# Sorting the first of five transpose tasks of each attention head one slot group later, in a kernel of attention, a routed expert layer and a max of three linear maps

## The chip, the core and the metric

The kernel runs on one core of a Trainium2 chip. The metric is the device time of one execution in microseconds (us). Five engines work side by side, each through its own queue in order: TensorE (PE: matmuls and transposes; its weight loads are listed as PEld), VectorE (DVE), ScalarE (ACT), GpSimd (POOL) and SyncE (SP, which issues DMA transfers). An engine that reaches an instruction whose input is not ready waits there, and all that is queued behind it waits too. Transfers are also issued by GpSimd (the indirect ones, which gather rows by a list of indices).

## The reference

All data is fp32. The sizes are batch 4, 8 heads, 576 positions, head size 64; a token is one position of one batch, 2304 in all, of 512 elements.

```
scores = q k^T / 8 + cum[i] - cum[j]          cum = cumsum(log f), causal
attn   = exp(scores - rowmax) / rowsum        out = attn v
x      = out as 2304 tokens of 512 (8 heads x 64)
e      = argmax over 8 experts of cosine(x, expert_emb) / tau, gate = its softmax weight
x      = gate * (relu(x w1[e]) w2[e])         512 -> 1024 -> 512
h      = max(x m1, x m2, x m3)                512 -> 768
result = h w_out                              768 -> 512
```

## The kernel before

**Heads and row blocks.** The 32 heads (4 batches x 8) are taken two at a time as 16 pairs p; head h is 2p or 2p+1. The 576 rows of a head are cut into row blocks t = 0 to 4. Block 0 holds the last 64 rows left over and is made for both heads of a pair at once; block t = 1 to 4 has 128 rows and, being causal, 128 t + 64 columns: 192, 320, 448 and 576. For each block, TensorE makes the scores (`s_h_t_k`, lines 421 and 426, two passes each; block 4 in two halves of 288 columns), VectorE adds the mask and takes the row extreme (`P_h_t` and `nm`, lines 448 and 454), ScalarE makes the exponential in place with its row sum (line 480), TensorE transposes the block in squares of 128 (`t_h_t<-swap,P_h_t`, line 500), and ScalarE or VectorE evicts the squares to `PT` (`PT<-t`, lines 535 for VectorE and 537 for ScalarE).

**The remainders.** The 64 columns of each block beyond the squares of 128 are transposed apart, all four of a head into one tile of its own, `tl_h` (one buffer). Those of blocks 1 to 3 stand in the same task as that block's squares and ahead of them (line 498, `tl_h<-ident,P_h_t`). The one of block 4 is a task by itself, called t = 0 in the code (line 494, `tl_h<-ident,P_h_4`): it allocates the tile, and the tasks of blocks 1 to 3 name it as something they come after. When all four are in, one eviction copies them to `PT` (`PT<-tl_h`).

**After a pair.** VectorE adds up the row sums (`sum_p`, line 547). GpSimd copies them with the two halves of the partitions exchanged (`rs_p`, lines 552 and 553), and VectorE takes the reciprocal of `rs_p` in place (line 556). TensorE multiplies by V (`po_p_u`, line 570, u = 0 and 1), the result is evicted (`ot_p_u`), transposed back by a matmul (`pb_p_u`, line 590), and VectorE multiplies it by the reciprocal (line 599). SP stores it to `x_dram` (line 610).

**The early expert.** One expert's share of the tokens of the first three batches is worked on before all of attention is done. A small matmul, `p3` (line 886), counts; ten small VectorE instructions on its result (lines 889 to 917) end in a list of indices, `gidxe`; GpSimd gathers the rows (two indirect transfers `V0<-x_dram,gidxe`, line 645), SP loads that expert's weights (`we0`, `we1` and a spare tile, line 682), VectorE and ScalarE split the weights into a rounded part and the rest (into `At1`, `Bt1`, `R11`, `R21`, `At2`, `Bt2`, lines 535, 537 and 690), TensorE transposes the gathered rows (`xe`, line 651, evicted to `xs0` and `xs1`), and `pe0` (line 1239) is the first matmul of the expert stage. Later gathers of the other experts' tokens are called `gat` (line 1405).

**What sets the order.** Nothing of attention is written in the order in which it is issued. Each step is a task with a list of engines that may do it, an estimated cost, a priority, the tasks it comes after and the buffers it needs. A small greedy scheduler in the kernel's own code (class `Sched`) keeps a clock for each engine in its estimates; again and again it takes, of the tasks that are ready, the one that can start first by its clocks, and among those that can start alike the one with the lowest priority. The program is emitted in that order. The buffers that it counts are three for score tiles `s`, two for transposed squares `t`, one for `tl`, two for `po` and `pb` together, eight for `P`. Priorities are slots: `slot[h, t]` is 5 h + i for the i-th of the order 4, 0, 3, 1, 2, scores have `slot - 2`, transposes have `slot + 3` (`LT` is 3), a pair's closing steps have 10 p + 20 and a little more.

Of the kernel before, what the change touches and what calls it, by code (L numbers as in the profile page):

```python
# [266 lines left out]
def attention(tc, g, qT, kT, v, x_dram, es):  # L267
# [79 lines left out]
    sd = Sched({"s": 3, "P": NPB, "t": 2, "tl": 1, "o": 2, "ot": 2}, 9.0)  # L347
# [5 lines left out]
    LEAD, LT, LO = 2, 3, 10  # L353
    order = (4, 0, 3, 1, 2)
    slot = {(h, t): 5 * h + i for h in range(NH) for i, t in enumerate(order)}
    side, ready, fs, fr, fe, ft, fv, ftv, fo, fb, fn_ = {}, {0: []}, {}, {}, {}, {}, {}, {}, {}, {}, {}
# [55 lines left out]
    def s_task(h, t, k, j0, w):  # L412
        p, r = divmod(h, 2)
        i = p % NQ

        def fn(e):
            st = st_[h, t, k] = ps_s.tile([128, 512], F32, tag="s", name=f"s_{h}_{t}_{k}")
            wp = max(w, 192)
            for ps_i, (lt, rt, kk) in enumerate(((At[i], R1[i], 128), (Bt[i] if p else At[i], R2[i], 66 if p else 128))):
                if t == 0:  # L420
                    nc.tensor.matmul(st[:, 0:192].rearrange("p (r j) -> p r j", r=2), lt[0:kk].rearrange("p r q -> p (r q)")[:, S - 64:S + 64],
                                     rt[0:kk, :, 0:96],
                                     start=(ps_i == 0), stop=(p > 0 and ps_i == 1))
                    continue
                q0 = ROW0[t] - (0 if r else 64)
                nc.tensor.matmul(st[:, 0:wp], lt[0:kk, r, q0:q0 + 128],  # L426
                                 rt[0:kk, r, j0:j0 + wp], start=(ps_i == 0), stop=(p > 0 and ps_i == 1))
            if p == 0 and t == 0:
                for x in range(2):
                    nc.tensor.matmul(st[:, 96 * x:96 * x + 96], g.pick[:, x], g.cc[:, 0:96], start=False, stop=(x == 1))  # L430
            elif p == 0:
                nc.tensor.matmul(st[:, 0:wp], g.pick[:, r], g.cc[:, j0:j0 + wp], start=False, stop=True)

        fs[h, t, k] = sd.task("PE", pe(2 * max(w, 192)), fn, slot[h, t] - LEAD, side.get(h, []), get=("s", (h, t, k)))

    def r_task(h, t, k, j0, w, n, ext):
        def fn(e):
            if k == 0:
                if t == order[0] and h % H == 0:
                    b = h // H  # L440
                    sums[b] = sm.tile([128, NBLK, H], F32, tag="sums", name=f"sums{b}", bufs=2)
                    nc.vector.memset(sums[b][:, 0, :], 1.0)
                P = pp.tile([128, S], F32, tag="P", name=f"P_{h}_{t}")
                nm = sm.tile([128, 2], F32, tag="nm", name=f"nm_{h}_{t}")
                Pt[h, t] = P, nm
            P, nm = Pt[h, t]
            if t == 0:
                nc.vector.tensor_tensor_reduce(out=P[:, 0:128].rearrange("p (r j) -> p r j", r=2),
                                               in0=st_.pop((h, t, k))[:, 0:192].rearrange("p (r j) -> p r j", r=2)[:, :, 0:64],
                                               in1=g.mask2, scale=-0.125, scalar=3.0e38, op0=ALU.add, op1=ALU.min,  # L450
                                               accum_out=nm[:, 0:1])
                return
            m0 = S - ext + j0
            nc.vector.tensor_tensor_reduce(out=P[0:n, j0:j0 + w], in0=st_.pop((h, t, k))[0:n, 0:w], in1=g.mask[0:n, m0:m0 + w],  # L454
                                           scale=-0.125, scalar=(3.0e38 if k == 0 else nm[0:n, 0:1]),
                                           op0=ALU.add, op1=ALU.min, accum_out=nm[0:n, k:k + 1])

        deps = [fs[h, t, k]] + ([fr[h, t]] if k else [])
        fr[h, t] = sd.task("DVE", dve(w), fn, slot[h, t], deps, get=None if k else ("P", (h, t)), rel=[("s", (h, t, k))])
# [3 lines left out]
    def head(h):  # L463
        p, r = divmod(h, 2)
        b = h // H
        T = PT[h % NPT]
        for t in order:
            n, ext = ROWS[t], EXT[t]
            if t == 0:
                n, ext = 128, 128  # L470
                if r == 0:
                    continue
            parts = ((0, 288), (288, 288)) if t == 4 else ((0, ext),)
            for k, (j0, w) in enumerate(parts):
                s_task(h, t, k, j0, w)
                r_task(h, t, k, j0, w, n, ext)

            def exp(e, t=t, n=n, ext=ext, k=len(parts) - 1, c=h % H):
                P, nm = Pt[h, t]
                nc.scalar.activation(out=P[0:n, 0:ext], in_=P[0:n, 0:ext], func=AF.Exp, bias=nm[0:n, k:k + 1], scale=-1.0,  # L480
                                     accum_out=sums[b][0:n, t, c:c + 1])

            fe[h, t] = sd.task("ACT", 0.28 + ext / 1200, exp, slot[h, t], [fr[h, t]])
            if t == 0:
                fe[h - 1, 0], fs[h - 1, 0, 0] = fe[h, 0], fs[h, 0, 0]
        old = [fo[p - 2]] if p >= 2 else []
        for t in order:
            i0 = ROW0[t]

            def tr(e, t=t, i0=i0):  # L490
                P = Pt.pop((h, t))[0] if t not in (0, 4) else Pt[h, 4][0]
                if t == 0:
                    tl = tl_[h] = ps_t.tile([128, 512], F32, tag="tl", name=f"tl_{h}", bufs=1)
                    nc.tensor.transpose(tl[0:64, 3 * LAP:4 * LAP], Pt.pop((h, 4))[0][0:LAP, 512:576], g.ident[0:LAP, 0:LAP])
                    return
                w = tl_[h, t] = ps_t.tile([128, 512], F32, tag="t", name=f"t_{h}_{t}")
                if t != 4:
                    nc.tensor.transpose(tl_[h][0:64, LAP * t - LAP:LAP * t], P[0:LAP, 128 * t:128 * t + 64], g.ident[0:LAP, 0:LAP])
                for a in range(t):
                    nc.tensor.transpose(w[:, 128 * a:128 * a + 128], P[:, 128 * a:128 * a + 128], g.swap)  # L500
                if t == 1 and r:
                    nc.tensor.transpose(w[:, 128:256], Pt.pop((h, 0))[0][:, 0:128], g.ident)

            nb = {0: 0.6, 1: 1.6 + r, 2: 2.6, 3: 3.6, 4: 4}[t]
            deps = [fe[h, 4]] if t == 0 else [fe[h, t]] + ([ft[h, 0]] if t != 4 else []) + ([fe[h, 0]] if t == 1 and r else [])
            ft[h, t] = sd.task("PE", 0.107 * nb, tr, slot[h, t] + LT, deps, get=("tl", h) if t == 0 else ("t", (h, t)),
                               rel=[("P", (h, x)) for x in {0: (4,), 1: (0, 1) if r else (1,), 4: ()}.get(t, (t,))])
            if t == 0:
                continue

            def ev(e, t=t, i0=i0):
                w = tl_.pop((h, t))
                if t == 1 and r:
                    for x in range(2):
                        evict(e, PT[(h - 1 + x) % NPT][0:64, 0, 0:64], w[low[x], 128 + 64 * x:192 + 64 * x])
                evict(e, T[:, 0:t, i0:i0 + 128], w[:, 0:128 * t].rearrange("p (a i) -> p a i", a=t))

            x = 0.26 if t == 1 and r else 0.0
            fv[h, t] = sd.task(("ACT", "DVE"), (act(128 * t) + x, dve(128 * t) + x), ev, slot[h, t] + LT - 4, [ft[h, t]] + old,
                               rel=[("t", (h, t))])  # L520

        def tail(e):
            d = T[0:64, 1, 128:192]
            dst = bass.AP(tensor=d.tensor, offset=d.offset, ap=[list(d.ap[0]), [S + 128, 4], [1, 64]])
            evict(e, dst, tl_.pop(h)[0:64, 0:4 * LAP].rearrange("p (a i) -> p a i", i=LAP)[:, :, 0:64])

        fv[h, 0] = sd.task(("ACT", "DVE"), (act(256), dve(256)), tail, slot[h, order[-1]] + LT - 4,
                           [ft[h, t] for t in order] + old, rel=[("tl", h)])
# [4 lines left out]
    def evict(e, out, in_):  # L533
        if e == "DVE":
            nc.vector.tensor_copy(out, in_)  # L535
        else:
            nc.scalar.activation(out=out, in_=in_, func=AF.Copy)
# [1336 lines left out]
```

## Time and profile before

| | before |
|---|---|
| median of 3 runs (lowest to highest) | 723.43 us (723.03 to 724.41) |
| the profiled execution, its own time | 724.2 us |
| its span, first to last instruction | 722.5 us |
| TensorE busy | 98% of the span, 4699 instructions |
| VectorE, ScalarE, GpSimd busy | 60%, 52%, 22% |
| mean granted TensorE clock | 0.998 of full speed |

The trace is of one execution. Busy time is the time in which an engine had at least one instruction under way; a row of the timeline gives the start, the duration, the engine, the line, the operation with what it writes and reads (buffer numbers left out, so that `s_31_3` and `s_30_2` are both `s`), the shapes and a count where alike rows follow each other. In brackets behind it stands how long the engine sat idle just before, and what ended that.

### The profile page before, as it was taken

How to read it: one execution, taken by the hardware profiler on the slowest of the kernel's cores; microseconds unless marked ns; L12 is line 12 of the kernel's file. 1: busy time of each engine (PE TensorE's matmuls, PEld its weight loads, DVE VectorE, ACT ScalarE, POOL GpSimd, SP SyncE). 2: the span in 40 equal slices, each digit the busy share in tenths (PEclk: the TensorE clock that was granted, in tenths of full speed). 3: DMA queues.
4: the chain of work that ended last, by engine and by line, in shares of the span. 5: the costliest groups of instructions: out<-in, count | busy, mean ns of one | idle time of the engine just before them, and what ended most of it. 6: DMA issues, size and time to landing. Idle time of an engine off the chain costs nothing. (4 is left out here: it accounts for less than half of the span.)

```text
span 722.5 us, 12938 instructions
## 1 busy us (share of the span) xinstructions
PE 708.6 (98%) x4699; PEld 642.4 (89%) x4699; DVE 436.8 (60%) x1108; ACT 373.2 (52%) x860; POOL 155.5 (22%) x203
## 2 busy tenths in 40 slices
PE   8999999999999999999999999999999999999996
PEld 7788897888999999999999999888888888888994
DVE  7978988888888987778976779412302221221220
ACT  7899989998577555566565544311211121122111
POOL 7895565741020101102100000100020011002001
PEclk9999999999999999999999999999999999999999
DMA  7779586725366665656656423000010000001001
GB/s 241 240 223 273 133 242 188 200 49 165 95 205 212 213 220 185 216 195 230 194 192 222 164 80 116 30 15 0 1 59 0 1 30 29 1 0 46 14 1 46
DMA packets 44764, 89.77 MB, mean 124 GB/s; under 512 B 23320, under 2 KB 23320, under 8 KB 44696
## 3 DMA queue, kind: packets, MB, share of 16 engines
q1 hardware_dynamic: 41144, 79.10, 34.6%
q0 software_dynamic: 3520, 9.78, 3.9%
q8 instruction: 39, 0.64, 0.4%
q14 instruction: 29, 0.24, 0.1%
q10 hardware_dynamic: 32, 0.02, 0.0%
HBM read 74.87 MB, written 9.44 MB: 117 GB/s over the span
## 5 line engine op out<-in xcount | busy, mean ns | idle before, releaser
L1640 DVE TENSOR_TENSOR tm<-pm,tm 128x512 f32<-128x512 f32 (+1 forms) x60 | 38.3, 638 | 177.9 <-PE pm L1241 177.5
L1241 PE MATMUL pm<-y,m 128*128 128x512 f32 (+1 forms) x288 | 108.1, 375 | 0.0
L1239 PE MATMUL pm<-y,m 128*128 128x512 f32 (+1 forms) x288 | 108.1, 375 | 0.0
L1240 PE MATMUL pm<-y,m 128*128 128x512 f32 (+1 forms) x288 | 108.1, 375 | 0.0
L1682 POOL DMA_INDIRECT out_dram<-oo,ctidx x18 | 17.8, 988 | 336.9 <-ACT oo L1679 333.9
L480 ACT ACTIVATE P<-P,nm 128x576 f32<-128x576 f32 (+2 forms) x144 | 84.0, 587 | 2.8 <-DVE nm L454 1.3
L1295 DVE TENSOR_TENSOR w<-stg,w 128x1024 fp32r<-128x1024 f32 x60 | 73.0, 1221 | 20.3 <-ACT w L1278 19.4
L1278 ACT ACTIVATE g<-tm 128x512 fp32r<-128x512 f32 (+1 forms) x30 | 17.7, 590 | 114.6 <-DVE tm L1640 114.6
L1278 ACT ACTIVATE w<-stg 128x1024 fp32r<-128x1024 f32 x56 | 59.0, 1056 | 21.8 <-DMA stg<-in_w_dram 10.9
L1239 PE MATMUL py<-h,w 128*128 128x256 f32 (+6 forms) x224 | 68.7, 307 | 0.0
L1239 PE MATMUL ph<-x,w 128*128 128x256 f32 (+6 forms) x224 | 67.8, 303 | 0.0
L1240 PE MATMUL ph<-x,w 128*128 128x256 f32 (+6 forms) x224 | 67.7, 302 | 0.0
L1241 PE MATMUL py<-h,w 128*128 128x256 f32 (+6 forms) x224 | 67.6, 302 | 0.0
L1241 PE MATMUL ph<-x,w 128*128 128x256 f32 (+6 forms) x224 | 67.6, 302 | 0.0
L1240 PE MATMUL py<-h,w 128*128 128x256 f32 (+6 forms) x224 | 67.5, 301 | 0.0
L426 PE MATMUL s<-R,At 128*128 128x288 f32 (+3 forms) x170 | 60.2, 368 | 2.4 <-DVE nm L454 1.1
L454 DVE CUSTOM_DVE_ANT_0 P<-s,mask 128x288 f32<-128x288 f32 (+3 forms) x128 | 58.6, 475 | 6.0 <-PE s L426 2.2
L1241 PEld LDWEIGHTS pm<-y,m 128*128 128x128 f32 x288 | 54.1, 188 | 8.5
L1240 PEld LDWEIGHTS pm<-y,m 128*128 128x128 f32 x288 | 54.0, 188 | 8.5
L1239 PEld LDWEIGHTS pm<-y,m 128*128 128x128 f32 x288 | 54.1, 188 | 8.4
L1405 POOL DMA_INDIRECT gat<-x_dram,gidx x20 | 23.3, 1166 | 158.1 <-PE xt L1412 133.4
L500 PE MATMUL t<-swap,P 128*128 128x128 f32 x320 | 55.7, 275 | 0.3 <-DVE PT L535 0.2
(385 smaller groups left out, 1748.7 us busy)
## 6 DMA issues: line engine op xcount, KB each, us to landing
stg<-in_w_dram SPq DMA_DIRECT2D x60, 512.0 KB
sd<-in_m_dram SPq DMA_DIRECT2D x18, 512.0 KB
q<-in_q_dram SPq DMA_DIRECT2D x15, 576.0 KB
k<-in_k_dram SPq DMA_DIRECT2D x15, 576.0 KB
Bt<-At SPq DMA_DIRECT2D x15, 288.0 KB
V<-in_v_dram SPq DMA_DIRECT2D x8, 512.0 KB
x_dram<-XL SPq DMA_DIRECT2D x64, 64.0 KB
sd_o<-in_mo_dram SPq DMA_DIRECT2D x6, 512.0 KB
```

The costliest lines, as they stand in the source:

```text
L426: nc.tensor.matmul(st[:, 0:wp], lt[0:kk, r, q0:q0 + 128], rt[0:kk, r, j0:j0 + wp], start=(ps_i == 0), stop=(p > 0 and ps_i == 1))
L454: nc.vector.tensor_tensor_reduce(out=P[0:n, j0:j0 + w], in0=st_.pop((h, t, k))[0:n, 0:w], in1=g.mask[0:n, m0:m0 + w], scale=-0.125, scalar ...
L480: nc.scalar.activation(out=P[0:n, 0:ext], in_=P[0:n, 0:ext], func=AF.Exp, bias=nm[0:n, k:k + 1], scale=-1.0, accum_out=sums[b][0:n, t, c:c ...
L500: nc.tensor.transpose(w[:, 128 * a:128 * a + 128], P[:, 128 * a:128 * a + 128], g.swap)
L1239: nc.tensor.matmul(out, whi, xhi, start=start, stop=False)
L1240: nc.tensor.matmul(out, whi, xlo, start=False, stop=False)
L1241: nc.tensor.matmul(out, wlo, xhi, start=False, stop=stop)
L1278: nc.scalar.activation(out=out, in_=in_, func=AF.Copy)
L1295: ENG[e].tensor_tensor(out=w[:, 1], in0=t, in1=w[:, 0].bitcast(F32), op=ALU.subtract)
L1405: nc.gpsimd.indirect_dma_start(out=t[0:n], out_offset=None, in_=x_dram, in_offset=bass.IndirectOffsetOnAxis(ap=idx, axis=0))
L1640: nc.vector.tensor_tensor(out=mx[0], in0=mx["p", w][:, 0:MC], in1=mx[0], op=ALU.max)
L1682: nc.gpsimd.indirect_dma_start(out=out, out_offset=bass.IndirectOffsetOnAxis(ap=g.sidx[:, col:col + 1], axis=0), in_=o[1], in_offset=None, ...
```

## The change

The task of block 4's remainder had the priority `slot[h, 0] + 3`, the second of its head. It gets that of block 3's transposes, `slot[h, 3] + 3`, plus 0.2. All the rest of the code is as it was.

```
             nb = {0: 0.6, 1: 1.6 + r, 2: 2.6, 3: 3.6, 4: 4}[t]
             deps = [fe[h, 4]] if t == 0 else [fe[h, t]] + ([ft[h, 0]] if t != 4 else []) + ...
-            ft[h, t] = sd.task("PE", 0.107 * nb, tr, slot[h, t] + LT, deps, get=...
+            ft[h, t] = sd.task("PE", 0.107 * nb, tr, slot[h, t or 3] + LT + (0.2 if t == 0 else 0.0), deps, get=...
```

The order on TensorE, between the scores of head 5 and the transposes of head 4. The number at the end of a name counts tiles. Before:

```order
L421 MATMUL s_5_0_0_638<-R12_127,At2_120 128x192
L421 MATMUL s_5_0_0_638<-R22_130,Bt2_123 128x192
L494 MATMUL tl_4_641<-ident_75,P_4_4_540 64x66
L426 MATMUL s_5_3_0_644<-R12_127,At2_120 128x448
L426 MATMUL s_5_3_0_644<-R22_130,Bt2_123 128x448
L498 MATMUL tl_4_641<-ident_75,P_4_3_560 64x66
L500 MATMUL t_4_3_648<-swap_187,P_4_3_560 128x128 x3
```

The same place of the change:

```order
L421 MATMUL s_5_0_0_638<-R12_127,At2_120 128x192
L421 MATMUL s_5_0_0_638<-R22_130,Bt2_123 128x192
L426 MATMUL s_5_3_0_641<-R12_127,At2_120 128x448
L426 MATMUL s_5_3_0_641<-R22_130,Bt2_123 128x448
L494 MATMUL tl_4_646<-ident_75,P_4_4_540 64x66
L498 MATMUL tl_4_646<-ident_75,P_4_3_560 64x66
L500 MATMUL t_4_3_648<-swap_187,P_4_3_560 128x128 x3
```

The remainder of block 4 moved behind the scores of `s_5_3` and now stands directly ahead of block 3's remainder. Up to head 13 nothing else moves on TensorE; from head 14 on the scheduler's clocks differ enough that other tasks change places as well.

Late in attention, on TensorE, around `p3`. Before:

```order
L426 MATMUL s_29_4_1_2997<-R12_127,At2_120 128x288
L426 MATMUL s_29_4_1_2997<-R22_130,Bt2_123 128x288
L500 MATMUL t_28_4_3003<-swap_187,P_28_4_2912 128x128 x4
L886 LDWEIGHTS ones_793
L886 MATMUL p3_3009<-ohs_799,ones_793 128x8
L421 MATMUL s_29_0_0_3011<-R12_127,At2_120 128x192
L421 MATMUL s_29_0_0_3011<-R22_130,Bt2_123 128x192
L494 MATMUL tl_28_3015<-ident_75,P_28_4_2912 64x66
L426 MATMUL s_29_3_0_3019<-R12_127,At2_120 128x448
L426 MATMUL s_29_3_0_3019<-R22_130,Bt2_123 128x448
```

In the change:

```order
L426 MATMUL s_29_2_0_3046<-R12_127,At2_120 128x320
L426 MATMUL s_29_2_0_3046<-R22_130,Bt2_123 128x320
L426 MATMUL s_30_4_0_3053<-R10_125,At0_118 128x288
L426 MATMUL s_30_4_0_3053<-R20_128,Bt0_121 128x288
L426 MATMUL s_30_4_1_3059<-R10_125,At0_118 128x288
L426 MATMUL s_30_4_1_3059<-R20_128,Bt0_121 128x288
L886 LDWEIGHTS ones_793
L886 MATMUL p3_3062<-ohs_799,ones_793 128x8
L500 MATMUL t_29_4_3067<-swap_187,P_29_4_2941 128x128 x4
```

`p3` moved from between heads 28 and 29 to behind the first scores of head 30: more of attention's matmuls stand ahead of it, and fewer behind it.

On VectorE, around the reciprocal of `rs_14` (pair 14 is heads 28 and 29; a `P` of head 31 is that head's mask and row extreme, and `nm` its second output). Before:

```order
L547 TENSOR_SCALAR sum_14_3197<-sums3_2492 128x10
L448 ISA P_31_0_3200,nm_31_0_3201<-s_31_0_0_3191,mask2_179 128x128
L448 ISA nm_31_0_3201 128x1
L535 CAST At1_119<-we0_3081 128x512
L454 ISA P_31_3_3218,nm_31_3_3219<-s_31_3_0_3194,mask_78 128x448
L454 ISA nm_31_3_3219 128x1
L454 ISA P_31_1_3241,nm_31_1_3242<-s_31_1_0_3203,mask_78 128x192
L454 ISA nm_31_1_3242 128x1
L454 ISA P_31_2_3245,nm_31_2_3246<-s_31_2_0_3215,mask_78 128x320
L454 ISA nm_31_2_3246 128x1
L556 RECIPROCAL rs_14_3206<-rs_14_3206 128x10
L535 CAST At1_119<-we0_3081 128x512
```

In the change:

```order
L547 TENSOR_SCALAR sum_14_3178<-sums3_2503 128x10
L556 RECIPROCAL rs_14_3181<-rs_14_3181 128x10
L535 COPY ot_14_1_3194<-po_14_1_3157 128x256
L535 CAST At1_119<-we0_3137 128x512
L454 ISA P_31_4_3211,nm_31_4_3212<-s_31_4_0_3189,mask_78 128x288
L454 ISA nm_31_4_3212 128x1
L454 ISA P_31_4_3211,nm_31_4_3212<-s_31_4_1_3201,mask_78,nm_31_4_3212 128x288
L454 ISA nm_31_4_3212 128x1
L448 ISA P_31_0_3226,nm_31_0_3227<-s_31_0_0_3214,mask2_179 128x128
L448 ISA nm_31_0_3227 128x1
L690 TENSOR_TENSOR Bt1_122<-we0_3137,At1_119 128x512
```

The reciprocal moved from behind all of head 31's row extremes to ahead of them, directly behind the sum.

On GpSimd the order is the same in both. Here is the change's, with what each waits for in brackets (DMASW are the queues of the indirect transfers, DMAHW those of SP's):

```order
L645 DMA V0_135<-x_dram_65,gidxe_3114 128x512 [waits DMAHW5_49,DMAHW4_49,DMAHW6_49,DMAHW1_49,DMAHW7_49,DMAHW0_49,DVE_49]
L645 DMA V0_135<-x_dram_65,gidxe_3114 128x512
L552 COPY rs_14_3181<-sum_14_3178 64x10 [waits DMASW1_49,DMASW0_49,DVE_49]
L552 COPY rs_14_3181<-sum_14_3178 64x10
L553 COPY rs_14_3181<-sum_14_3178 64x1 [waits Pool_49]
```

What moved is not here: the copy that fills `rs_14` stands behind both gathers and waits for their queues and for VectorE's sum, before and after the change alike.

## Rows read from the trace of the kernel before

**Rows 1.** The page, parts 1 and 5: busy time; the row-extreme group.

```profile
PE 708.6 (98%) x4699; PEld 642.4 (89%) x4699; DVE 436.8 (60%) x1108; ACT 373.2 (52%) x860; POOL 155.5 (22%) x203
...
L454 DVE CUSTOM_DVE_ANT_0 P<-s,mask 128x288 f32<-128x288 f32 (+3 forms) x128 | 58.6, 475 | 6.0 <-PE s L426 2.2
```

**Rows 2.** Timeline of PE: `s_31_3`, `po_14` and the first row of `pe0`.

```profile
173.36 0.39 PE L426 MATMUL s<-R,At 128*128 128x448 f32 x1
...
174.82 2.94 PE L570 MATMUL po<-PT,V 128*64 128x320 f32 x32
...
187.21 0.38 PE L1239 MATMUL pe<-xs,At 128*128 128x256 f32 x1
```

**Rows 3.** Windows of PE: stretch, length, busy (instructions), clock, DMA share, GB/s.

```profile
88.00:160.00 72.00, 70.81 (x650) 1.00 0.62 172
173.36:187.21 13.85, 13.39 (x121) 1.00 0.42 133
```

**Rows 4.** Timeline of POOL, 164 to 180 us.

```profile
167.74 1.24 POOL L645 DMA_INDIRECT V<-x_dram,gidxe  x1 [5.31 <-PE t L500]
169.29 0.95 POOL L645 DMA_INDIRECT V<-x_dram,gidxe  x1 [0.31 <-issue]
176.95 0.43 POOL L552 COPY rs<-sum 64x10 f32<-64x10 f32 x2 [6.71 <-DMA V<-x_dram,gidxe]
```

**Rows 5.** Timeline of DVE: the reciprocal of `rs_14`.

```profile
177.66 0.22 DVE L556 RECIPROCAL rs<-rs 128x10 f32<-128x10 f32 x1 [1.91 <-POOL rs L553]
```

**Rows 6.** Timeline of PE: remainder alone (102 us) and with a pair (112 us).

```profile
102.31 0.60 PE L500 MATMUL t<-swap,P 128*128 128x128 f32 x4
102.75 0.22 PE L494 MATMUL tl<-ident,P 66*64 66x66 f32 x1
...
103.33 0.50 PE L500 MATMUL t<-swap,P 128*128 128x128 f32 x3
...
112.65 0.60 PE L500 MATMUL t<-swap,P 128*128 128x128 f32 x4
...
113.50 0.22 PE L494 MATMUL tl<-ident,P 66*64 66x66 f32 x1
...
113.62 0.50 PE L500 MATMUL t<-swap,P 128*128 128x128 f32 x3
```

**Rows 7.** Timeline of PE from `p3` on.

```profile
164.45 0.17 PE L886 MATMUL p<-ohs,ones 128*128 128x8 f16 x1
164.48 0.33 PE L421 MATMUL s<-R,At 128*128 128x192 f32 x1
...
166.05 0.90 PE L590 MATMUL pb<-w,ot 128*128 128x144 f32 x6
166.78 0.22 PE L498 MATMUL tl<-ident,P 66*64 66x66 f32 x1
...
167.50 0.66 PE L590 MATMUL pb<-w,ot 128*128 128x144 f32 x4
167.90 0.40 PE L426 MATMUL s<-R,At 128*128 128x320 f32 x1
...
168.29 0.22 PE L494 MATMUL tl<-ident,P 66*64 66x66 f32 x1
168.66 0.37 PE L426 MATMUL s<-R,At 128*128 128x288 f32 x1 [0.15 <-DVE nm L454]
...
169.37 0.25 PE L498 MATMUL tl<-ident,P 66*64 66x66 f32 x1
```

**Rows 8.** The tile V's gathers: from issue to landing.

```profile
DMA to landing us min/median/max: 7.5/7.6/7.8
```

**Rows 9.** Timeline of ACT: exp of `P_31_4`, and the eviction of `tl_31`.

```profile
174.81 0.77 ACT L480 ACTIVATE P<-P,nm 128x576 f32<-128x576 f32 x1
...
182.95 0.37 ACT L537 ACTIVATE PT<-tl 64x256 f32<-64x256 f32 x1
```

**Rows 10.** The tile gat, the later gathers: from issue to landing.

```profile
DMA to landing us min/median/max: 3.0/4.5/8.8
```

More of the change, by code (lines that the diff above doesn't have):

```diff
@@ L505, in head @@
             deps = [fe[h, 4]] if t == 0 else [fe[h, t]] + ([ft[h, 0]] if t != 4 else []) + ([fe[h, 0]] if t == 1 and r else [])
-            ft[h, t] = sd.task("PE", 0.107 * nb, tr, slot[h, t] + LT, deps, get=("tl", h) if t == 0 else ("t", (h, t)),
+            ft[h, t] = sd.task("PE", 0.107 * nb, tr, slot[h, t or 3] + LT + (0.2 if t == 0 else 0.0), deps, get=("tl", h) if t == 0 else ("t", (h, t)),
                                rel=[("P", (h, x)) for x in {0: (4,), 1: (0, 1) if r else (1,), 4: ()}.get(t, (t,))])
```

## The prediction

> **What bounds the kernel now.** I read the page first, then the instructions in order of time on TensorE, VectorE, ScalarE and GpSimd, from 95 us to 190 us, and last the idle time by stretch. The page gives TensorE 98% of the span [rows 1]. So the order in which its queue is served is the time: the attention stage ends for it where `pe0`, the first matmul of the expert stage, starts (187.21 us, [rows 2]), and from there it works on to the tail. What moves `pe0` moves the end, and I find no later place with idle time to take up a shift. In attention it hardly waits: from 88 to 160 us it is idle for 1.2 us of 72 [rows 3].
>
> The reader is to see one more thing. Two gathers on GpSimd start at 167.74 and 169.29, and the next GpSimd instruction, a 0.2 us copy that swaps the halves of `rs_14`, starts at 176.95: it sat idle 6.71 us until the gather's DMA landed [rows 4]. The built order says the same in both kernels: `rs_14`'s copy waits for both gathers. VectorE's reciprocal of `rs_14` then starts at 177.66, after 1.91 us of idling [rows 5]. Before the change this cost little, because the reciprocal stood behind all of head 31's softmax.
>
> **The change, part by part.**
>
> *The pairing itself.* Before the change, 20 of the 32 remainders `tl_h<-P_h_4` stand alone ahead of an `s_.._3` pair, and 19 of these follow either four transposes (8) or an `s_.._0` pair (11). In the change 25 stand beside `P_h_3`'s remainder. For odd heads both forms are in the trace: from the four transposes to the group of three it is 102.31 to 103.33, 1.02 us, with the remainder alone, and 112.65 to 113.62, 0.97 us, with it paired [rows 6]. That is 0.05 us each. For even heads no paired case stands in the same surroundings; the bounds are 0 and the 0.05 of the odd ones, and I take 0.03, as the row ahead is a matmul longer than a transpose's slot. Sum: 8 x 0.05 + 11 x 0.03 = 0.73 us gained, at most 0.95.
>
> *What the scheduler makes of it.* The new sort key does more than move 20 small rows: from head 14 on the planner's choices differ on TensorE, VectorE and ScalarE. Most of these exchanges are the same work in another order. TensorE idles only 1.2 us between 88 and 160 [rows 3], so I price them at 0, from -1.2 (all waits gone) to +1.2 (doubled).
>
> *`p3` comes later.* `p3` opens the chain that picks the early expert: `p3`, ten small VectorE instructions, the two gathers and the weight loads on SP. It started at 164.45. In the change the work of heads 28 to 30 that followed it, from 164.48 to 169.37, stands ahead of it, except `pb_13_0` (166.05 to 166.78), the four transposes of `t_29_4` (four slots of 0.11, the quarter of the 0.44 between 102.31 and 102.75), `pb_13_1` (167.50 to 167.90) and `tl_29` (168.29 to 168.66): 4.89 - 0.73 - 0.44 - 0.40 - 0.37 = 2.95 us [rows 6, 7]. With the pairing's gain `p3` starts at 164.45 + 2.95 - 0.73 = 166.67.
>
> *The reciprocal of `rs_14` comes earlier in its queue.* From `p3` to the reciprocal it took 177.66 - 164.45 = 13.2 us [rows 5, 7]; nearly all is issue of the gathers and their landing, 7.5 to 7.8 us after issue [rows 8]. The gathers and the SP loads issued beside them hang on the same chain, so I keep 13.2: the reciprocal starts at 179.9. But in the change `ot_14_1`, a cast of `At1` and the whole softmax of head 31 are queued behind it. Score tiles have three buffers: `s_31_4_0`, `s_31_4_1` and `s_31_0` take them, and `s_31_3` needs the one that VectorE's `P_31_4` frees. That is 0.2 us for the reciprocal, and three instructions that I put at 0.4 each, by the 475 ns mean of the score reductions [rows 1]: `s_31_3` starts at `p3` + 14.6.
>
> TensorE is there long before. Its way from `p3` to `s_31_3` was 173.36 - 164.45 = 8.91 [rows 2, 7]; in the change `po_14` (2.94) stands in it and the 2.95 have gone ahead, so 8.9 again. It stands idle for 5.7 us, in a place where it did not wait.
>
> *What is late next.* Head 31's exponentials wait too. ScalarE's row exp for `P_31_4` begins one 0.5 us reduction later, at `p3` + 15.1. From that instruction to the last eviction `PT3<-tl_31`, ScalarE took 174.81 to 183.32, 8.5 us over 22 rows [rows 9]. In the change five of those (`R11`, `ot_14_0`, one `xs0`, two `At2`; 2.57 us) stand elsewhere and two evictions come in (0.55): 6.5 us back to back. Before, TensorE had `po_14` to do meanwhile; now nothing. From the last eviction to `pe0` it was 187.21 - 183.32 = 3.9 us [rows 2, 9], and that stays. `pe0` starts at 166.67 + 15.1 + 6.5 + 3.9 = 192.2, against 187.21: 5.0 us later. If ScalarE were no limit, TensorE's own rows would be: from `s_31_3` to `pe0` 13.85, less `po_14` 2.94 and less the 0.46 that it idles there [rows 3], 10.45 us, so 191.7 and 4.5 later. I take 5.0, as ScalarE's queue is full from the first exp on.
>
> *Sum.* The profiled execution took 724.2 us, its span 722.5 and 1.7 around it; the median of the runs is 723.43. The span becomes 727.5, the profiled execution 729.2, the median **728.4 us**, 0.7% more. A measurement of this kernel tells 0.2% (1.4 us) from no change.
>
> **Rivals.**
>
> *The gathers land sooner.* Later gathers of the same size in this kernel land in 3.0 to 8.8 us, median 4.5 [rows 10]. With 3.0 the reciprocal starts 4.6 us earlier, the whole row above shifts with it, and `pe0` comes 0.4 us late: 723.8, no change; with 4.5 it is 725.3. For it: the spread. Against it: both early gathers took 7.5 to 7.8 while 512 KB weight loads ran beside them, and those are still issued beside them. The Trainium skill, page "DMA: Bandwidth & Descriptors", section "Anatomy of one DMA — SWDGE (gpsimd) path", fits such a DMA as 2.0 us plus its bytes over 436 KB per us, an estimated 2.6 us for 256 KB. By that rule the change would end near 723.4, no change; the two measured landings speak against it here.
>
> *The swap is not held by the gathers.* If GpSimd's copy waited for something else until 176.95, the reciprocal has its input at once, VectorE never stops, and only the good sides are left: `p3` at 166.67, the way from it to `pe0` 22.76 less the 2.95 gone ahead, 186.5, and up to 1 us less for the wait at the end of `po_14`, which now lies earlier. That is 721.7 to 722.7, faster. It decides if GpSimd's copy starts before TensorE reaches `s_31_3`, `p3` + 8.9. Against it: the order names the gathers' queues in that wait.
>
> *More waits.* Slots for transposes number two, so TensorE and ScalarE may take turns in head 31, and the stretch to 160 us may lose its 1.2: 729.6 to 731.
>
> **How the numbers follow.** Forecast, the reciprocal blocks VectorE: 0.70, on its own 726 to 730. Gathers land sooner: 0.12, a third of it still over 0.2% slower. Swap not held: 0.08. More waits: 0.10. Slower by over 0.2%: 0.70 + 0.10 + 0.04 = 0.84; within: 0.08 from the sooner landings and 0.02 of the swap's case, 0.10; faster 0.06. The range leaves out the swap's case, the part of the sooner landings within 0.2%, and the top of the last case: 724.9 to 730.7.
>
> **What would show it.** Right: in the after profile GpSimd's `rs` copy waits some 7 to 9 us for the gather's DMA; VectorE's reciprocal has over 5 us idle ahead of it; the `s` matmul 128x448 of head 31 starts some 14.6 us after `p3` with some 6 us of idle time; `pe` begins near 192. Wrong: `p3` not later than 165, landings under 5 us, or a reciprocal that idles under 2 us. Transposes with a pair of remainders should show the 0.97 us step in most heads. What happens after `pe0` should last as long as before; if it doesn't, the sum fails there.

## The result, and the profile after

The changed kernel takes 730.15 us (median of 5 runs, 729.87 to 731.97), the kernel before 723.43 us (5 runs, 723.03 to 724.41): 1.0102 times as long, 95% interval 1.0091 to 1.0113. The profiled execution took 729.92 us with a span of 728.2 us, 5.7 more than before. The forecast was 728.4 us; the direction and the place were right, and the loss was larger than forecast: 6.7 us by the medians where 5.0 stood, and by the ratio 723.43 x 1.0102 = 730.8 us, just above the range's upper end of 730.7.

First the page of the changed kernel, its busy times, beside [rows 1]:

```profile
PE 709.0 (97%) x4699; PEld 643.6 (88%) x4699; DVE 436.1 (60%) x1108; ACT 372.9 (51%) x860; POOL 157.9 (22%) x203
```

TensorE does the same work in the same busy time. What grew is idle time, and it sits in one place. GpSimd's timeline, beside [rows 4]:

```profile
168.96 1.24 POOL L645 DMA_INDIRECT V<-x_dram,gidxe  x1 [8.13 <-DVE gidxe L917]
...
178.12 0.43 POOL L552 COPY rs<-sum 64x10 f32<-64x10 f32 x2 [6.66 <-DMA V<-x_dram,gidxe]
```

VectorE's timeline, beside [rows 5]: the sum of pair 14, the reciprocal, and the first row extreme of head 31.

```profile
171.44 0.16 DVE L547 TENSOR_SCALAR sum<-sums 128x10 f32<-128x10 f32 x1
178.83 0.22 DVE L556 RECIPROCAL rs<-rs 128x10 f32<-128x10 f32 x1 [7.23 <-POOL rs L553]
...
179.57 0.45 DVE L454 CUSTOM_DVE_ANT_0 P<-s,mask 128x288 f32<-128x288 f32 x1
```

GpSimd's copy waits for the gathers as long as before. But VectorE now stands for 7.23 us in front of the reciprocal (1.91 before), and head 31's extremes stand behind it. TensorE's timeline, beside [rows 2, 7]:

```profile
166.24 0.18 PE L886 MATMUL p<-ohs,ones 128*128 128x8 f16 x1
...
170.37 2.94 PE L570 MATMUL po<-PT,V 128*64 128x320 f32 x32
...
174.64 0.49 PE L500 MATMUL t<-swap,P 128*128 128x128 f32 x3
180.09 0.74 PE L426 MATMUL s<-R,At 128*128 128x448 f32 x1 [4.95 <-DVE nm L454]
180.62 0.58 PE L426 MATMUL s<-R,Bt 66*128 66x448 f32 x1
...
194.01 0.38 PE L1239 MATMUL pe<-xs,At 128*128 128x256 f32 x1
```

`s_31_3` starts with 4.95 us of idle time. Then comes what the forecast didn't have: the same matmul that took 0.39 us before [rows 2] takes 0.74. The windows of TensorE (stretch, length, busy and instructions, granted clock, DMA share, GB/s) say why:

```profile
174.90:180.09 5.19, 0.24 (x4) 0.85 0.84 283
180.09:183.00 2.91, 2.91 (x12) 0.50 0.00 0
183.00:186.00 3.00, 3.00 (x18) 0.60 0.04 9
186.00:194.00 8.00, 6.69 (x60) 1.00 0.15 36
```

In the 5.19 us before, TensorE was busy for 0.24. In the 3 us behind it the granted clock is 0.50, the lower of its two levels (1.2 GHz). The 0.60 of the next 3 us is a mean: 2.4 us at 0.50 and 0.6 at 1.00 give it, so the clock is full again (2.4 GHz) from about 185.4 us on, 5.3 us after `s_31_3` began. Over the whole span that shows as 0.993 against 0.998. `pe0` starts at 194.01, 6.80 later than before.

### The profile page after: what moved, and what is told of

Same layout as the page of the kernel before. It is cut to its first block, busy times and chain, and to the rows that moved or that the text cites. A ratio compares the mean times of both kernels' runs of the same rounds, so it can differ in the third digit from the quotient of the medians.

```text
span 728.2 us, 12931 instructions
## 1 busy us (share of the span) xinstructions
PE 709.0 (97%) x4699; PEld 643.6 (88%) x4699; DVE 436.1 (60%) x1108; ACT 372.9 (51%) x860; POOL 157.9 (22%) x203
```

## The experiments

The runs are from three chips. All times are set against the kernel before on the same chip (its medians there were 723.28, 723.53 and 724.25 us), so the ratios are what to compare; the changed kernel's is 1.0102.

**One instruction put back.** The reciprocal of `rs_14` is emitted behind head 31's last row extreme, all else is the change's order.

```diff
-            nc.vector.reciprocal(rs[0], rs[0])
+            nc.vector.reciprocal(rs[0], rs[0]) if p != NP - 2 else held.append(rs)
...
-                                           op0=ALU.add, op1=ALU.min, accum_out=nm[0:n, k:k + 1])
+                                           ...); (h, t) == (NH - 1, 2) and nc.vector.reciprocal(held[0][0], held[0][0])
```

> The change with one instruction moved: the reciprocal of rs_14 stands behind head 31's last row extreme on VectorE, as before the change; the order on all other engines is the change's. If the blocked VectorE is the cause: GpSimd's copy still waits some 6.7 us for the gathers, but s_31_3 starts near 175.2 us without a wait, the granted clock stays 1.00, pe0 starts near 186.4, and the time is 722 to 723 us, at or a little below the kernel before. If the reshuffled order or the later p3 is the cause: no change against the changed kernel, 729 to 731 us.

Measured: 723.28 us, ratio 1.0001 (0.9993 to 1.0010). Its timeline of TensorE, `s_31_3` and `pe0`:

```profile
174.73 0.45 PE L426 MATMUL s<-R,At 128*128 128x448 f32 x1
...
186.21 0.38 PE L1239 MATMUL pe<-xs,At 128*128 128x256 f32 x1
```

No wait, and `pe0` 7.80 us earlier than in the changed kernel, although GpSimd's copy waited for the gathers as ever (6.83 us). Of the 7.80, 5.36 are the later start of `s_31_3` (180.09 against 174.73) and 2.44 the longer way from there to `pe0` (13.92 against 11.48). The whole loss hangs on the place of one 0.22 us instruction; the rest of the new order costs nothing. `pe0` is even 1.00 us earlier here than in the kernel before, but that did not reach the time: further on in the profiled execution, at 190.21, TensorE stands 0.92 us for VectorE in front of a small matmul (line 847), where the kernel before did not wait.

**Its input made sooner.** The reciprocal stays where the change put it, but ScalarE makes the three copies of `rs_14`.

```diff
-                nc.gpsimd.tensor_copy(rs[0][low[x]], rs[1][low[1 - x]])
+                evict("ACT", rs[0][low[x]], rs[1][low[1 - x]]) if p == NP - 2 else nc.gpsimd.tensor_copy(rs[0][low[x]], rs[1][low[1 - x]])
```

(The third copy, of one column, likewise.)

> The change with only the engine of rs_14's three copies changed: ScalarE makes them instead of GpSimd, so that they don't stand behind the gathers. If it is the wait for the gathers that reaches VectorE through the reciprocal: the reciprocal runs near 172 us with under 1 us of idle time ahead of it although it stands ahead of head 31's extremes, pe0 starts near 186.5 to 187 (some 0.6 us of copies more on ScalarE), 722 to 723.5 us. If the place of the reciprocal matters by itself, or the reshuffle does: 729 to 731 us.

Measured: 722.39 us, ratio 0.9987 (0.9978 to 0.9996). VectorE's row:

```profile
172.88 0.22 DVE L556 RECIPROCAL rs<-rs 128x10 f32<-128x10 f32 x1 [1.32 <-ACT rs L537]
```

So the early place does no harm by itself; waiting for the gathers does. The two together are called the trap below. The idle time of 1.32 us was above the "under 1" expected, and `pe0` at 186.34 shows that it was hidden. This kernel is faster than the one before, by 0.13%.

**The same copies in the kernel before.** The same edit on the kernel before:

> The kernel before with rs_14's three copies on ScalarE instead of GpSimd. Beside e2_swap_act, which is the same on the change, it tells what the change is worth once the wait for the gathers is out of both. If that wait cost the kernel before nothing, since the reciprocal stood behind head 31's extremes: 723.0 to 723.8 us, and the change gains 0.7 to 1.3 us beside it. If the copies' wait also held something in the kernel before (the casts and splits of weights behind the reciprocal): 722 to 722.8 us, and the change is worth nothing in itself.

Measured: ratio 1.0003 (0.9994 to 1.0012). There the wait cost nothing that shows; the prediction had said little. Beside this run the change with ScalarE's copies is worth the difference, 0.16%, some 1.2 us (`pe0` stands at 187.48 here and at 186.34 there). With the reciprocal put back it was worth nothing that shows, so what the change gains without its trap lies between 0 and 0.16%.

**The trap set in the kernel before.** Its reciprocal of `rs_14` is emitted directly behind GpSimd's copies, in all else the old order.

```diff
-            nc.gpsimd.tensor_copy(rs[0][low[0], 0, 0:1], rs[1][low[0], 0, 1:2])
+            nc.gpsimd.tensor_copy(rs[0][low[0], 0, 0:1], rs[1][low[0], 0, 1:2]); p == NP - 2 and nc.vector.reciprocal(rs[0], rs[0])
```

> The kernel before, with only the reciprocal of rs_14 moved up on VectorE, to behind P_31_0 and ahead of the cast of At1 and the extremes of blocks 3, 1 and 2 of head 31. If the blocked VectorE is the cause, the old order must suffer too: those extremes start near 178 instead of 174.4 us; TensorE still gets s_31_3 and s_31_1 done and stands before s_31_2 for up to 3.5 us, ScalarE's exponentials come as late: 726.5 to 729 us, more if the granted clock falls after the idle time. If the reshuffled order is what costs: 723.4 us as before.

Measured: 725.80 us, ratio 1.0036 (1.0023 to 1.0049): slower, by less than expected. VectorE's reciprocal had 3.57 us of idle time, and TensorE's rows with waits are others than were expected:

```profile
178.87 0.66 PE L651 MATMUL xe<-ident,V 128*128 128x128 f32 x4 [0.25 <-DVE nm L454]
...
181.48 1.00 PE L590 MATMUL pb<-w,ot 128*128 128x144 f32 x6 [1.96 <-ACT ot L537]
```

With two extremes of `P_31_4` and that of `P_31_0` done ahead of the reciprocal, all three score buffers were free, and `s_31_2` did not wait; `po_14` then covered most of the stop, and ScalarE's late exponentials came through only as 1.96 us ahead of `pb`. The granted clock stayed 1.00 on both sides of that wait. The wait for the gathers is the same in both orders; what stands behind it in the queue decides the price.

**The clock.** In the changed kernel's order, matmuls whose result nothing uses are put ahead of `s_31_3`, into columns of `tl_30` that nothing reads.

```diff
-            st = st_[h, t, k] = ps_s.tile([128, 512], F32, tag="s", name=f"s_{h}_{t}_{k}")
+            (h, t) == (NH - 1, 3) and [nc.tensor.matmul(tl_[NH - 2][:, 384:512], g.ident, g.ident, start=True, stop=True) for _ in range(48)]; st = ...
```

> The change with 48 matmuls of 128 columns ahead of s_31_3 on TensorE, which write unused columns of the tile tl_30; their result is used by nothing. They fill the 5 us in which TensorE stood idle. If half clock after the idle time is a cost of its own: the granted clock stays 1.00, the way from s_31_3 to pe0 falls from 13.9 to some 11.2 us, and the time is 727 to 728 us. If ScalarE's queue or VectorE's sets that stretch, so that TensorE's pace there is hidden: 13.9 us remain and the time is 729.5 to 731 us.

Measured: 732.88 us, ratio 1.0131, a miss of the design: one such matmul shows as two rows of 0.11 us, the 48 took 10.88 us in place of 5, and `s_31_3` started at 185.61. But the clock stayed full, and from there to `pe0` it took 11.41 us. With 23 of them:

> As e4_fill, but with 23 of the matmuls, since one of them took 0.22 us there and not the 0.11 that was reckoned: 23 x 0.222 = 5.1 us, the length of the idle time. s_31_3 starts at 180.1 us as in the changed kernel. If half clock is a cost of its own: granted clock 1.00 throughout, from s_31_3 to pe0 11.2 to 11.5 us instead of 13.9, pe0 near 191.5, time 2.3 to 2.7 us under the changed kernel's, 727.3 to 728.0. If VectorE's and ScalarE's queues set the pace there and TensorE's is hidden: pe0 stays near 194 and the time within 0.7 us of the changed kernel's.

Measured: 728.75 us, ratio 1.0058 (1.0044 to 1.0072). TensorE's timeline:

```profile
174.89 5.30 PE L417 MATMUL tl<-ident 128*128 128x128 f32 x46
179.98 0.47 PE L426 MATMUL s<-R,At 128*128 128x448 f32 x1
...
191.83 0.38 PE L1239 MATMUL pe<-xs,At 128*128 128x256 f32 x1
```

and its windows:

```profile
174.90:180.00 5.10, 5.10 (x49) 1.00 0.84 279
180.00:183.00 3.00, 3.00 (x24) 1.00 0.00 0
```

`s_31_3` is as late as in the changed kernel, but its way to `pe0` is 11.85 us instead of 13.92 (11.2 to 11.5 had been expected). The half clock behind the idle time cost 2.1 us of its own, and keeping TensorE at work on nothing gave them back.

**What makes the gathers late.** Two tries. First, the two loads into the spare tile go behind pair 14's first store:

```diff
-                nc.sync.dma_start(out=raw[q], in_=g.w1[bass.ds(er[0], 1), q].rearrange("o p c -> (o p) c"))
+                go = lambda: nc.sync.dma_start(out=raw[q], in_=...); held.append(go) if q > 1 else go()
...
-                nc.sync.dma_start(out=dst[r0:r0 + ROWS[t]], in_=X[0:ROWS[t], t])
+                nc.sync.dma_start(out=dst[r0:r0 + ROWS[t]], in_=X[0:ROWS[t], t]); (p, t) == (NP - 2, 0) and [go() for go in held]
```

> The change with the two weight loads into the spare tile issued on SP behind the first store of pair 14 instead of beside the gathers: 1 MB less moves while the gathers are under way. If the gathers land late because they share the DMA engines with the loads: they land 4 to 5.5 us after issue instead of 6.1 to 7.5, GpSimd's copy and the reciprocal start 1.5 to 3 us earlier (near 176.5), TensorE's idle time shrinks by as much to 2 to 3.5 us; the time falls by at least that, to 726 to 728.5 us, unless the later spare loads hold up the matmuls that need them. If the 7 us are the gathers' own: the reciprocal stays at 178.8 and the time at 730.

Measured: 731.07 us, ratio 1.0088 (1.0074 to 1.0101); the gathers landed 6.8 to 7.2 us after issue and the reciprocal came at 178.44. These landings lie within the 6.1 to 7.5 of the changed kernel, so the theory that these two loads hold the gathers up fell. Second, `we0`, `we1` and the first spare load, which stood ahead of pair 13's stores, go behind them (`q < 3`, and pair 13's last store as the place):

> The change with the three weight loads that stood ahead of pair 13's stores on SP (we0, we1, the first spare) issued behind these stores, some 3 us later, so that the gathers have the DMA engines nearly to themselves at first. If the loads hold up the gathers: they land 3 to 5 us after issue, GpSimd's copy starts near 174 to 175 us instead of 178.1, and the time falls by 2 to 4 us against the changed kernel, unless the later we0 holds VectorE's cast, which stands directly behind the reciprocal. If the 7 us are the gathers' own: copy at 178 and 730 to 731 us.

Measured: 727.67 us, ratio 1.0052 (1.0037 to 1.0067), from four executions between 725.68 and 728.32, of which the slowest is the profiled one. The tile V's gathers, and GpSimd's row:

```profile
DMA to landing us min/median/max: 3.8/4.3/4.8
```

```profile
175.35 0.43 POOL L552 COPY rs<-sum 64x10 f32<-64x10 f32 x2 [4.01 <-DMA V<-x_dram,gidxe]
```

So the loads issued beside the gathers (SP issues `we0` and `we1` at 169.24 in the changed kernel and at 172.37 here) take some 3 us of the 7, and the loss shrinks with them. TensorE's windows around `s_31_3` in this run, which starts at 177.70 after 2.69 us of idle time:

```profile
174.70:177.70 3.00, 0.31 (x4) 0.95 1.03 377
177.70:182.00 4.30, 4.30 (x18) 0.50 0.49 200
```

Here, too, half clock follows the idle time, and the way from `s_31_3` to `pe0` (192.21) is 14.51 us, longer than in the changed kernel: `pe0` is only 1.80 us earlier although GpSimd's copy started 2.77 us earlier. In the kernel before with the early reciprocal 1.96 us of idle time did not bring half clock.

**The pairing alone.** The kernel before with its order untouched; block 4's remainder is emitted by block 3's task, in all 32 heads.

```diff
-                if t == 0:
+                if t == 0: return
+                if t == 3:
                     tl = tl_[h] = ps_t.tile([128, 512], F32, tag="tl", name=f"tl_{h}", bufs=1)
                     nc.tensor.transpose(tl[0:64, 3 * LAP:4 * LAP], ...)
-                    return
```

> The kernel before, its scheduler's order untouched, with block 4's remainder and the allocation of tl emitted at the head of block 3's transposes in every head, 32 of 32. The pairing alone, without any other task moved. By the forecast's sum of 0.05 us for odd and 0.03 for even heads: p3 starts some 0.7 us earlier (163.7 instead of 164.45), and the time is 722.4 to 723.0 us, 0.4 to 1.0 under the kernel before. If a remainder costs the same alone as in a pair: p3 at 164.4 and 723.4 us.

Measured: 723.87 us, ratio 0.9996 (0.9987 to 1.0005), not to be told from no change by the time. In the trace `p3` starts at 164.00 and `pe0` at 186.78, 0.45 and 0.43 us earlier than before: 22 more remainders stand in a pair there, so 0.02 us came out for each.

**The scheduler told of the wait.** The changed kernel with other estimates for the two gathers: the second is said to take 8.0 us of GpSimd's clock (1.3 before), and the times until their data count as there become 8.0 and 0.2 us (3.0 before).

```diff
-            ga = sd.task("Pool", 1.3, gather, 10 * (NP - 3), [chosen, fo[NP - 5]], lat=3.0)
+            ga = sd.task("Pool", (1.3, 8.0)[c], gather, 10 * (NP - 3), [chosen, fo[NP - 5]], lat=(8.0, 0.2)[c])
```

> The change with one more number changed: the scheduler is told that GpSimd is taken for 8.0 us by the second gather (1.3 before, and 3.0 of latency that did not hold GpSimd's clock). Nothing of the work differs; rs_14's copies still wait for the gathers, but the scheduler plans for it and puts the reciprocal and what hangs on it behind head 31's extremes by itself. If the wait that the scheduler did not know is the cause: reciprocal without harm, s_31_3 near 175 without a wait, 722 to 724 us. If a reciprocal behind a gather is not what decides: 729 to 731 us.

Measured: 722.44 us, ratio 0.9990 (0.9981 to 0.9999). The reciprocal went behind head 31's extremes without being told to, and `s_31_3` and `pe0` stand at 174.79 and 186.25:

```profile
174.79 0.45 PE L426 MATMUL s<-R,At 128*128 128x448 f32 x1
...
186.25 0.38 PE L1239 MATMUL pe<-xs,At 128*128 128x256 f32 x1
```

**The good parts together.** The change with ScalarE's copies and all 32 pairs, beside a second run of the version with the copies alone:

> The change with rs_14's copies on ScalarE (as e2_swap_act) and every remainder of block 4 emitted at the head of block 3's transposes (as e5_pair_only), 32 of 32. If the wait for the gathers is the one thing wrong with the change and pairing gains a few hundredths each: 0.1 to 0.3 per cent faster than the kernel before, 1 to 2 us. If e2's gain came by accident of one order and pairing gives nothing: within 0.1 per cent of the kernel before.

> The same kernel as e2_swap_act, beside e10_best on one chip: 0.05 to 0.2 per cent under the kernel before, and e10_best at or up to 0.2 us below it.

Measured: 722.55 us, ratio 0.9993 (0.9984 to 1.0002), and 722.43 us, ratio 0.9988 (0.9979 to 0.9997). The three pairs more that the change lacked add nothing that shows, and 0.1 to 0.3% had been expected. The gain of some 0.1% over the kernel before repeats for the version with the copies alone; the interval of the version with all pairs includes no change.

## Why the prediction was right or wrong

**The pairing.** The count of pairs in the forecast was off: by the built order 10 remainders of block 4 stand directly ahead of block 3's before and 29 in the change, not 25. The price of a step was right. In the trace of the changed kernel the step from the four transposes to the group of three is 0.96 or 0.97 us in most odd heads, as said (1.01 to 1.05 with the remainder alone), and from the four transposes over an `s_.._0` pair to the group of three it is 1.19 us in most even heads (1.21 or 1.22 alone), 0.03 less. Yet with the pairing alone only 0.45 us arrived at `p3` for 22 pairs, where 0.73 was reckoned for 19; what took the rest back is not shown.

**The order.** Priced at 0 from -1.2 to +1.2. With the reciprocal put back, the whole is as fast as before, so the price holds for the time. TensorE's idle time between 88 and 160 us fell from 1.19 to 0.30 us.

**`p3`.** Forecast 166.67, measured 166.24, 0.43 earlier.

**The reciprocal.** Forecast `p3` + 13.2, measured + 12.6 (178.83 - 166.24); the first row extreme, the buffer and `s_31_3` follow as said, at + 13.85 instead of 14.6. The idle time was 4.95 us where 5.7 stood.

**The way from `s_31_3` to `pe0`.** This is the step that failed. The forecast had 10.9 us: 0.5 to the exponential of `P_31_4`, 6.5 for ScalarE's queue to the last eviction, 3.9 from there. Measured were 13.92. ScalarE's two ends, and its longest wait between them:

```profile
180.74 0.78 ACT L480 ACTIVATE P<-P,nm 128x576 f32<-128x576 f32 x1 [5.62 <-DVE nm L454]
...
184.44 0.39 ACT L537 ACTIVATE PT<-t 128x256 f32<-128x256 f32 x1 [1.21 <-PE t L500]
...
188.91 0.38 ACT L537 ACTIVATE PT<-tl 64x256 f32<-64x256 f32 x1
```

From the start of the first row to the end of the last, 189.29, that is 8.55 us for the middle term. The same two ends in the run with 23 filling matmuls:

```profile
180.63 0.78 ACT L480 ACTIVATE P<-P,nm 128x576 f32<-128x576 f32 x1 [5.60 <-DVE nm L454]
...
186.73 0.38 ACT L537 ACTIVATE PT<-tl 64x256 f32<-64x256 f32 x1
```

That is 6.48 us, which is the forecast's term, and with the reciprocal put back it is 6.46. The other 2.1 us are TensorE at half clock: ScalarE waited for its transposes. The forecast took TensorE's rows at the pace of the kernel before and noted a stall of 5.7 us without asking what it does to the clock; it put that cost at nothing. The Trainium skill, page "TensorE: Matmul & The Clock Gate", section "Part 1: The HAM clock gate", says of the clock: "the default state is throttled, and activity releases the throttle." The windows above agree: 0.50 behind the idle stretch, 1.00 when it was filled. The last term was 0.8 short: 4.72 us, in the changed kernel and with the reciprocal put back alike, since `pb_15` now waits 0.76 us for `ot_15`, which stands behind six casts of weights in ScalarE's queue. Only two of the six stood there before: the forecast took casts out of the middle term and let the last term "stay", while they had moved into it.

**After `pe0`.** "That stays" was off by 1.1 us in the other direction: 728.2 - 194.01 = 534.2 us against 535.3. TensorE's timeline of the kernel before has a wait that the changed kernel has not:

```profile
209.54 0.38 PE L1472 MATMUL ptl<-ident,hl 96*128 96x96 f32 x2 [0.74 <-ACT hl L1465]
```

This is no gain of the change. The wait (0.72 to 0.76 us) is there in all four profiled executions of variants on the chip where the kernel before has its median at 724.25 us, two in the old order and two in the new one, and in none of the eight on the other two chips (one in the old order, seven in the new one). So it goes with the chip or the execution; what causes it stays open. The profiled execution of the kernel before had it, and at 724.2 us it took 0.8 longer than its median.

**The sum.** In the profiled executions the terms add up: -0.43 (`p3`) - 0.75 (`s_31_3` at + 13.85 for + 14.6) + 3.0 - 1.1 = +0.7 on the forecast's span of 727.5, measured 728.2. That the span was missed by so little was luck. Between the medians the last term does not belong: 728.4 - 0.43 - 0.75 + 3.0 = 730.2 us, measured 730.15. The way from `s_31_3` to `pe0` is the whole miss, and two smaller errors hid a part of it.

**The rivals.** Sooner landings: it did not happen (6.1 to 7.5 us), but the condition was right, as 3.8 to 4.8 us with the loads out of the way, and a smaller loss, show. That loss was larger than this rival's price, though: 725.3 us stood for 4.5 us, and the ratio of 1.0052 is 727.2, with half clock behind the shorter idle time, too. The estimate of 2.6 us worked out from the Trainium skill, page "DMA: Bandwidth & Descriptors", section "Anatomy of one DMA — SWDGE (gpsimd) path", was met in neither state; the measurements decide. Swap not held: the changed kernel's 6.66 us decide against it; made true with ScalarE's copies, it gave 722.39 us, within the 721.7 to 722.7 of this rival. More waits: the measured time lies in its 729.6 to 731, but not by its mechanism. Between 88 and 160 us TensorE waited less, not more. In head 31 ScalarE did wait for TensorE's transposes (1.21 us above), but only at half clock: with TensorE kept at work those waits are gone and ScalarE's stretch is the forecast's. Why the framework has GpSimd's copy wait for two transfers whose data it doesn't touch was not settled.

## What to carry to other kernels

A priority that moves small tasks in a greedy plan is a new plan: look for instructions that moved forward in an in-order queue and whose input comes from an engine that waits for a transfer; the 0.22 us instruction is not the price, the queue behind it is. A plan can walk into a wait that its estimates don't hold; writing the wait into the estimate was here as good as any repair by hand. When a forecast has TensorE idle for several us, price the work behind it at half clock until rows show otherwise. And before a difference late in the trace is put down to a change, look whether it goes with the chip or the execution: 1.1 us did so here.

## Not expected of the hardware

After 4.95 us of idle time TensorE's granted clock was 0.50, and it was full again only some 5.3 us after TensorE went on; in the run with 2.69 us of idle time it fell as well, in the one with 1.96 us it did not. Filling the 5 us with matmuls that nobody needs made the kernel faster (ratio 1.0102 to 1.0058). Two gathers of 256 KB landed 6.1 to 8.5 us after issue with two or three loads of 512 KB issued beside them, and 3.8 to 4.8 us when these were issued some 3 us later.
